# A fused recurrence and token/channel mixer on one core: the same operations in another fixed order per engine

## The chip, the core and the metric

The kernel runs on one core of one Trainium2 chip. The metric is the device time of one execution in microseconds. Besides the times there is one profiled execution, with a trace of every instruction: TensorE (PE; its weight loads are shown as PEld), VectorE (DVE), ScalarE (ACT), GpSimd (POOL), SyncE (SP), and the DMA queues.

## What is computed

Four batches, eight heads, 768 positions, head size 48. A gated linear recurrence gives y, and y, with its heads side by side as 384 columns, goes through a mixer over positions (768 to 256 to 768) and one over channels (384 to 1536 to 384). Cut to what matters:

```python
f = 1.0 / (1.0 + np.exp(-f_logit))
for t in range(S):
    state = f[:, :, t, :, None] * state + np.einsum('bhd,bhe->bhde', k[:, :, t], v[:, :, t])
    y[:, :, t] = np.einsum('bhd,bhde->bhe', q[:, :, t], state)
...
xt = x.transpose(0, 2, 1)                      # x is y with heads joined
h = np.maximum(xt @ w_tok1, 0.0) @ w_tok2
u = x + h.transpose(0, 2, 1)
return u + np.maximum(u @ w_ch1, 0.0) @ w_ch2
```

Inputs and the output are fp32; the kernel computes with bf16 operands and fp32 sums.

## The kernel before

**Tiling.** Positions are cut into six chunks of 128 per batch. For a chunk, the logarithms of the gates (ScalarE: exp, then ln; lines 366 and 367, in batch 0 lines 387 and 383) are split into a high and a low bf16 part (the low one by a subtraction on GpSimd or VectorE, line 374, batch 0 line 396) and summed over positions by two matmuls with a triangle of ones (lines 456 and 457). ScalarE takes exp of the sums, once with each sign, into `GG` (lines 466 and 468); VectorE multiplies q and k by it (line 485, "product" in the prediction; batch 0 line 629) into `qk`; `qk` is transposed, for batches 0 to 2 by TensorE (line 495, batch 0 line 636) and a copy into `qkT`, for batch 3 by a DMA transpose on SP's queue (line 498). The scores of a chunk (line 408) are masked by VectorE into `AmT` (line 536); the state products k·v are line 424 (batch 0: line 657). The state goes on by `tsum` and `state` on VectorE (lines 547 and 549, 544 for the first chunk), with the chunk's last gate `glast`, which a small DMA on SP's queue lays out (line 476). Two copies "spread" each half of the state into the block-diagonal `state_bd` (ScalarE line 344 or GpSimd line 348). The result y of a chunk is one PSUM bank: state part (line 556) and masked scores times v (line 560). It is copied twice, to bf16 `x_bf` and fp32 `x_nat`. Batch 0 takes its chunks two at a time with masks for pairs (lines 607 to 736).

**Mixer.** Per batch: tok1 (line 750) with relu into `h1T`, tok2 (line 766), u added into `x_nat` (line 782) and cast to `u_bf`, six times three transposes into `uT` (line 798), 24 blocks ch1 of three matmuls (line 814), each relu'd by ScalarE (line 352) or VectorE (line 354) into `zT`, then per 128 positions three blocks ch2 of four matmuls (line 832), the sum (line 838) and the store (line 842).

**Order.** Nothing is scheduled when the kernel is built. The code makes a list of 1073 operations with their needs; the string `ORDER` says in which order they are recorded, and each engine takes its own in that order. In `ORDER` a token is an operation's number; a letter behind it chooses the engine where there is a choice (A ScalarE, D VectorE, G GpSimd); a number behind a colon is the PSUM bank (there are eight) that the operation opens; `z` and a number are that many idle matmuls (line 863), which only keep TensorE going. Engines, DMA queues and banks hence work strictly in the order of the list; an instruction that waits holds up all behind it on its engine. The numbers `kind` of each operation, among them the sizes for loads, are for the program that searches orders; they change no instruction.

**Loads.** GpSimd issues the loads of q, k, v and the weights (line 264, line 270), each with a descriptor run of its own in GpSimd's queue. Batches 1 and 2 have one load of the gate logits f and 18 of a chunk of k, q or v each; batch 3 has four, one each of f, k, q and v in one piece. Three load buffers for q, k, v and two for f turn round over the batches.

## Time and profile before

| | us |
|---|---|
| three runs | 175.95, 176.18, 178.95 |
| median | 176.18 |
| the profiled execution | 175.42 |
| its span, first to last instruction | 173.7 |
| TensorE busy | 165.0 |
| VectorE busy | 128.9 |
| ScalarE busy | 115.0 |
| GpSimd busy | 81.4 |

The profiled execution's own time holds 1.7 us outside the span. Times in the views are microseconds from the span's start. A row of a timeline has start, length, engine, line, operation, output and inputs, and how many equal instructions are merged; in brackets stands the engine's idle time just before it and what ended it. A row of a group has the line, form and count, then the busy time, the mean length of one in ns, and the idle time before the group with what ended it. Matmul records overlap, since the next one starts while the last still runs through the array.

### The profile page before, as it was taken

What the parts mean: (1) busy time and instruction counts of PE and PEld (TensorE: products, weight loads), DVE (VectorE), ACT (ScalarE), POOL (GpSimd) and SP (SyncE); (2) the same over time, 40 slices, a digit from 0 to 9 for tenths busy, and PEclk for the clock granted to TensorE, in tenths of its full rate; (3) what the DMA queues carried; (4) which work ended last, traced back from release to release, by engine and by line L of the source; (5) the groups of instructions that cost most, each with busy time, mean ns of one, the idle gap of its engine ahead of it and who ended that gap; (6) DMA issues with size and microseconds to landing.
All of it is one profiled execution on the core that took longest, in us unless ns stands there. A gap on an engine that the chain in (4) does not pass through costs nothing.

```text
span 173.7 us, 4503 instructions
## 1 busy us (share of the span) xinstructions
PE 165.0 (95%) x1795; PEld 104.5 (60%) x1795; DVE 128.9 (74%) x285; ACT 115.0 (66%) x258; POOL 81.4 (47%) x104
## 2 busy tenths in 40 slices
PE   6989988999999999999799999999999999999991
PEld 2466654656666766766567655666666657556660
DVE  7979985896798979799997967887938284555142
ACT  3999958999983598998958766797853234233000
POOL 2997814999772998999938401400000021000000
PEclk9999999999999999999999999999999999999999
DMA  5999999999999998999999968643270001210154
GB/s 142 228 170 177 250 209 199 142 99 189 162 137 236 95 107 186 165 158 125 79 143 133 107 33 101 207 84 86 41 131 0 0 0 49 109 72 0 38 193 183
DMA packets 84837, 21.56 MB, mean 124 GB/s; under 512 B 77552, under 2 KB 84000, under 8 KB 84816
## 3 DMA queue, kind: packets, MB, share of 16 engines
q0 software_dynamic: 69600, 13.77, 92.3%
q1 hardware_dynamic: 15216, 7.51, 17.2%
q8 instruction: 14, 0.23, 0.6%
q14 instruction: 7, 0.06, 0.1%
HBM read 25.17 MB, written 4.72 MB: 172 GB/s over the span
## 4 chain that ended last, share of the span: by engine, by line
PE 79%; ACT 10%; DVE 5%; DMA 2%; issue 1%; DVEq 0%; ACTq 0%
PE ps L832 26%; PE ps L814 24%; PE ps L750 5%; PE ps L766 4%; PE ps L408 3%; PE ps L798 2%; PE ps L495 2%; DMA f_sb<-in_f_logit_dram 2%; PE ps L863 2%; PE ps L560 2%; PE ps L456 2%; DVE zT L354 2%; PE ps L424 1%; PE ps L556 1%; ACT L L383 1%; ACT f_sb L387 1%
## 5 line engine op out<-in xcount | busy, mean ns | idle before, releaser
L832 PE MATMUL ps<-w_ch,zT 128*128 128x384 bf16 (+2 forms) x300 | 54.3, 319 | 0.0
L814 PE MATMUL ps<-uT,w_ch 128*128 128x384 bf16 x288 | 51.6, 326 | 1.0 <-DVE x_bf L346 1.0
L814 PEld LDWEIGHTS <-w_ch 128*128 128x128 bf16 x288 | 27.3, 98 | 18.3 <-issue 1.5
L832 PEld LDWEIGHTS <-zT 128*128 128x128 bf16 x300 | 27.7, 98 | 16.3 <-issue 0.4
L352 ACT ACTIVATE zT<-ps 128x384 bf16<-128x384 f32 x56 | 26.0, 498 | 13.7 <-PE ps L814 13.0
L354 DVE TENSOR_SCALAR zT<-ps 128x384 bf16<-128x384 f32 x40 | 21.1, 552 | 8.1 <-PE ps L814 7.4
L536 DVE TENSOR_TENSOR AmT<-ps,tri_bf 128x512 bf16<-128x512 f32 x36 | 23.5, 684 | 2.2 <-PE ps L408 2.2
L348 POOL CAST state_bd<-state 48x192 bf16<-48x192 f32 x18 | 6.5, 360 | 35.0 <-DVE state L549 16.5
L838 DVE TENSOR_TENSOR x_nat<-x_nat,ps 128x384 f32<-128x384 f32 (+2 forms) x25 | 13.1, 534 | 10.3 <-PE ps L832 9.9
L264 POOL DMA_DIRECT2D v_sb<-in_v_dram x16 | 15.9, 1000 | 1.3 <-DMA w_ch<-in_moe_w_ch_dram 1.0
L264 POOL DMA_DIRECT2D qk_sb<-in_q_dram x16 | 16.0, 999 | 0.1
L264 POOL DMA_DIRECT2D qk_sb<-in_k_dram x16 | 15.8, 996 | 0.2
L348 POOL CAST u_bf<-x_nat 128x384 bf16<-128x384 f32 x10 | 5.3, 532 | 19.9 <-DVE x_nat L782 19.9
L782 DVE TENSOR_TENSOR x_nat<-x_nat,ps 128x384 f32<-128x384 f32 x21 | 11.1, 549 | 3.5 <-PE ps L766 3.4
L750 PE MATMUL ps<-x_bf,w_tok 128*128 128x384 bf16 x48 | 13.5, 326 | 0.2 <-ACT x_bf L344 0.2
L374 POOL TENSOR_TENSOR Llo<-L 128x384 bf16<-128x384 f32 x13 | 11.0, 848 | 3.0 <-ACT L L367 2.8
L485 DVE TENSOR_TENSOR qk<-qk_sb,GG 128x768 bf16<-128x768 bf16 x18 | 11.5, 644 | 0.9 <-ACT GG L468 0.9
L344 ACT ACTIVATE state_bd<-state 48x192 bf16<-48x192 f32 x22 | 7.9, 360 | 6.2 <-DVE state L549 5.8
L863 PE MATMUL ps<-steady 128*128 128x512 bf16 x27 | 9.8, 476 | 1.5 <-DVE steady L279 1.5
L344 ACT ACTIVATE x_bf<-ps 128x384 bf16<-128x384 f32 x15 | 7.3, 487 | 5.5 <-DVE zT L698 2.0
L766 PE MATMUL ps<-h1T,w_tok 128*128 128x384 bf16 x48 | 10.2, 325 | 0.6 <-ACT h1T L352 0.6
L468 ACT ACTIVATE GG<-ps 128x384 bf16<-128x384 f32 x18 | 8.9, 496 | 0.5 <-PE ps L457 0.5
(99 smaller groups left out, 275.0 us busy)
## 6 DMA issues: line engine op xcount, KB each, us to landing
out_dram<-x_nat SPq DMA_DIRECT2D x23, 192.0 KB, 2.0
f_sb<-in_f_logit_dram POOLq DMA_DIRECT2D x3, 1152.0 KB, 11.3
f_sb<-in_f_logit_dram SPq DMA_DIRECT2D x3, 384.0 KB, 4.1
w_ch<-in_moe_w_ch_dram POOLq DMA_DIRECT2D x2, 576.0 KB, 11.5
qk_sb<-in_k_dram POOLq DMA_DIRECT2D x12, 96.0 KB, 4.5
qk_sb<-in_q_dram POOLq DMA_DIRECT2D x12, 96.0 KB, 5.0
v_sb<-in_v_dram POOLq DMA_DIRECT2D x12, 96.0 KB, 4.6
w_ch<-in_moe_w_ch_dram POOLq DMA_DIRECT2D x1, 1152.0 KB, 10.1
```

Source lines behind the costliest of these rows:

```text
L264: lambda eng=eng, into=into, of=of: eng.dma_start(out=into, in_=of),
L344: nc.scalar.activation(out_, in_, AF.Copy, bias=0.0, scale=1.0)
L348: nc.gpsimd.tensor_copy(out_, in_)
L352: nc.scalar.activation(out_, in_, AF.Relu, bias=0.0, scale=1.0)
L354: nc.vector.tensor_scalar(out_, in_, 0.0, None, ALU.max)
L536: add(("masked", b, c, p), DVE, lambda half=half, made=made: nc.vector.tensor_tensor(half, made(), tb4, ALU.mult), need=["tri_bf"], make=[ ...
L750: add(("tok1", b, rt, kt), PE, lambda rt=rt, kt=kt, pm=pm: nc.tensor.matmul(banks[pm.at][:, 0:DM], lhsT=w_tok1[:, kt, rt * 128:(rt + 1) * ...
L766: nc.tensor.matmul(banks[pm.at][:, 0:DM], lhsT=w_tok2[:, kt, tt * 128:(tt + 1) * 128], rhs=h1T[:, kt, :], start=(kt == 0 and not held), st ...
L814: nc.tensor.matmul(banks[pm.at][:, 0:384], lhsT=w[:, kt, c0:c0 + 128], rhs=uT[:, kt, cols], start=(kt == 0), stop=(kt == 2))
L832: nc.tensor.matmul(banks[pm.at][:, 0:n1 - n0], lhsT=zT[:, kt, tt * 128:(tt + 1) * 128], rhs=w_ch2[:, kt, n0:n1], start=(kt == 0), stop=(kt ...
L838: add(("sum", b, tt, n0), DVE, lambda un=un, pm=pm, n=n1 - n0: nc.vector.tensor_tensor(un, un, banks[pm.at][:, 0:n], ALU.add), make=[("x_n ...
L863: nc.tensor.matmul(banks[NBANK - 1], lhsT=steady[:, 0:128], rhs=steady, start=True, stop=True)
```

## The change

`ORDER` is replaced as a whole. It holds the same operations; one idle matmul more (28 for 27). Engines differ where there is a choice: of the two-way operations, six spreads of the state go from ScalarE to GpSimd; two copies of `qkT` and three of `uT` go from ScalarE to VectorE; two `x_bf` and two `x_nat` copies go from VectorE to ScalarE; one `u_bf` from ScalarE to GpSimd, one low part from GpSimd to VectorE, one relu of `h1T` and one of `zT` from ScalarE to VectorE, one u copy from VectorE to ScalarE. Banks are dealt anew. The order of the loads in GpSimd's queue changes (batch 3's k in one piece moves ahead of the last two q chunks of batch 2, for instance), and the stores of batches 0 and 1 stand later in SP's queue, all of them behind batch 3's first two transposes.

Some constants (`steady`, `inc2`, `exc2`, `half2`, `pmask`) lie in the buffer `x_nat[2]`, which is written as such only from batch 2 on, and no longer in tiles of their own. The rest are names and settings that choose what was chosen before (`NQ = 2`, `TURNED` with all six chunks of batch 3, `UTURN` empty) and the search's own numbers for a load in one piece (5900 for f, 5100 for the others).

```diff
+UTURN = ()
+NQ = 2
...
-TURNED = (3,)
+TURNED = {(3, 4), (3, 1), (3, 0), (3, 3), (3, 2), (3, 5)}
...
 ORDER = """
-32 33 13 17 34 20 5 10 18 21 6 14 22 0 7 1 9 36 12 15 49 23 35 26 2 3 28 51 24 25 37 50 53D 54 52D 39 27 z13 105:0 55
+32 33 21 22 11 34 5 7 17 14 19 0 15 1 35 12 20 24 23 49 6 2 36 3 4 26 28 18 50 25 39 8 51 52D 54 53D 37 27 z13 105:0
...
-1039 1070 1044 1071 1072 1050 804 1045 1051 570 1055 829 1046 1059 1047 1056 1040 1057 1060 1052 1041 1042 1061 1062
+1060 1070 1049 1071 1061 1072 1065 1062 1050 1066 829 1039 1051 1067 1045 1052 1040 824 1046 1047 1041 1042
...
-    def at(b, c):
+    def at(c):
 
-        return c % 2
+        return c % NQ
...
-            size = (1210 if n == "f" else 1150) if paired else (930 if n == "f" else 730) * many
+            size = (1210 if n == "f" else 1150) if paired else (930 if n == "f" else 730) * many if many < NCH else 5900 if n == "f" else 5100
...
-    steady = st([128, 512], BF16, "steady")
+    spare = x_nat[2].rearrange("p c n -> p (c n)").bitcast(BF16)
+    steady = spare[:, 0:512]
...
-        inc2 = st([128, C], BF16, "inc2")
-        exc2 = st([128, C], BF16, "exc2")
-        half2 = st([128, 2], BF16, "half2")
-        pmask = [st([128, C // 2, 2], BF16, f"pmask{j}") for j in range(2)]
+        inc2, exc2, half2 = spare[:, 512:640], spare[:, 640:768], spare[:, 1024:1026]
+        pmask = [spare[:, 768 + j * C:768 + (j + 1) * C].rearrange("p (t j) -> p t j", j=2) for j in range(2)]
...
-        if b in TURNED:
+        if (b, c) in TURNED:
...
+        if b in UTURN:
+            for tt in range(NCH):
+                add(("ut", b, tt), SP, lambda tt=tt: nc.sync.dma_start_transpose(
+                    out=uT[:, :, tt * 128:(tt + 1) * 128], in_=u_bf[:, tt, :]), need=[("u_bf", tt)],
+                    make=[("uT", tt, d) for d in range(3)], kind=("xfer", 700, 2700))
+        for th in range(0 if b in UTURN else 2):
```

## The prediction

> **What bounds the kernel now.** I read the page's shares first, then its slices, then the chain of waits, and then the timeline of each engine round the places where TensorE stops. The page gives the shape:

> ```profile
> span 173.7 us, 4503 instructions
> PE 165.0 (95%) x1795; PEld 104.5 (60%) x1795; DVE 128.9 (74%) x285; ACT 115.0 (66%) x258; POOL 81.4 (47%) x104
> PEclk9999999999999999999999999999999999999999
> ...
> L814 PE MATMUL ps<-uT,w_ch 128*128 128x384 bf16 x288 | 51.6, 326 | 1.0 <-DVE x_bf L346 1.0
> ...
> L485 DVE TENSOR_TENSOR qk<-qk_sb,GG 128x768 bf16<-128x768 bf16 x18 | 11.5, 644 | 0.9 <-ACT GG L468 0.9
> ```

> TensorE is busy for 95% of the span at a full granted clock, so an order can give back only its idle time: 173.7 - 165.0 = 8.7 us. That understates what its stops cost, since records of matmuls overlap. In the chain of waits (start, length, what):

> ```profile
> 19.47 0.65 PE ps L863 x3
> ...
> 148.81 8.78 PE ps L814 x54
> ...
> 169.84 0.56 DVE x_nat L838
> ```

> 54 matmuls in 8.78 us start every 0.163 us, and the page's row for line 814 gives one as 0.326 us long, so a stop shows 0.16 us less idle time than it costs. Three idle matmuls in 0.65 us are 0.22 us each. Behind the last matmul, from 169.8 on, lie 3.9 of the 8.7 us. The stops that I can name, from TensorE's timeline (start, length, what; in brackets the idle time and what ended it):

> ```profile
> 12.63 0.40 PE L636 MATMUL ps<-ident,qk 128*128 128x128 bf16 x4 [0.53 <-DVE qk L629]
> ...
> 22.96 0.30 PE L668 MATMUL ps<-zT 48*64 48x128 bf16 x6 [0.55 <-issue]
> ...
> 28.51 0.65 PE L766 MATMUL ps<-h1T,w_tok 128*128 128x384 bf16 x3 [0.65 <-ACT h1T L352]
> ...
> 75.19 0.62 PE L408 MATMUL ps<-qkT 48*128 48x128 bf16 x16 [0.17 <-ACT qkT L344]
> ...
> 85.90 0.65 PE L814 MATMUL ps<-uT,w_ch 128*128 128x384 bf16 x3 [1.00 <-DVE x_bf L346]
> ...
> 102.70 0.32 PE L750 MATMUL ps<-x_bf,w_tok 128*128 128x384 bf16 x1 [0.20 <-ACT x_bf L344]
> ```

> With 0.16 us added to each they cost 0.69, 0.71, 0.81, 0.33, 1.16 and 0.36 us, 4.1 us together. Behind 103 us nothing of that size is left. None is ended by a load. Who waited for the loads of line 264 at all:

> ```profile
> who waited for it (us, times):
>   ACT f_sb L387: 2.2, 1
>   DVE qk L629: 0.3, 1
> ```

> Both lines are batch 0's (387 and 629 stand in its code alone). No engine that computes waited for a load of batches 1 to 3. So what the new order was searched for, patience with the loads of batches 2 and 3, removes no stall of this execution; what counts is what else the new order does.

> **The change part by part.** Every operation stays; the new list has 28 idle matmuls for 27: +0.22 us.

> The stop at 12.63. The transposes of the second pair's q waited for a product on VectorE. TensorE's timeline just before it, and ScalarE's copy beside it:

> ```profile
> 10.31 0.32 PE L610 MATMUL ps<-Llo,inc 128*128 128x384 bf16 x1
> 10.67 0.44 PE L657 MATMUL ps<-v_sb,qk 64*64 64x48 bf16 x32
> 11.04 1.07 PE L636 MATMUL ps<-ident,qk 128*128 128x128 bf16 x16
> ```
> ```profile
> 11.92 1.02 ACT L344 ACTIVATE zT<-ps 128x1024 bf16<-128x1024 bf16 x1
> ```

> The new order does the first pair's 16 transposes (0.9 us from the first start to the last end's place in the stream) before the state products of line 657 (11.04 - 10.67 = 0.37), and then chunk 4's sums (4 x 0.163 = 0.65) and two score blocks, all ahead of the transposes that waited. So this wait goes. What is late next is the first score block, which needs the copy at 11.92: TensorE comes there at 10.31 + 0.16 + 0.9 + 0.22 (an idle matmul) + 0.37 + 0.65 = 12.6, and the copy ends at 12.94. I take 0.3 us of the 0.69 as left: -0.4 (bounds -0.69, and +0.3, were the copy to begin 0.6 us later than in the old order).

> The stop at 85.90 is the dearest. Line 814's block for batch 1 needs a PSUM bank that batch 2's first result holds until VectorE has copied it. VectorE then, and GpSimd beside it:

> ```profile
> 79.70 1.06 DVE L485 TENSOR_TENSOR qk<-qk_sb,GG 128x768 bf16<-128x768 bf16 x1
> ...
> 81.62 0.54 DVE L346 COPY x_nat<-ps 128x384 f32<-128x384 f32 x1
> 82.08 1.01 DVE L354 TENSOR_SCALAR zT<-ps 128x384 bf16<-128x384 f32 x2
> 83.01 1.07 DVE L485 TENSOR_TENSOR qk<-qk_sb,GG 128x768 bf16<-128x768 bf16 x1
> ...
> 84.48 0.90 DVE L549 TENSOR_TENSOR state<-tsum,glast 128x192 f32<-128x192 f32 x1
> 85.31 0.55 DVE L346 CAST x_bf<-ps 128x384 bf16<-128x384 f32 x1
> ```
> ```profile
> 79.53 0.82 POOL L374 TENSOR_TENSOR Llo<-L 128x384 bf16<-128x384 f32 x1
> 80.30 0.91 POOL L264 DMA_DIRECT2D v_sb<-in_v_dram  x1
> 81.21 3.09 POOL L264 DMA_DIRECT2D qk_sb<-in_q_dram  x2
> 84.30 0.86 POOL L374 TENSOR_TENSOR Llo<-L 128x384 bf16<-128x384 f32 x1
> ```

> VectorE runs without a gap (an operation starts some 0.08 us before the record of the last one ends), and from the fp32 copy of that bank at 81.62 to the bf16 one at 85.31 it is 3.7 us. A product of line 485 takes 1.06 here; its 18 took 11.5 us together, so the others are about 0.55. In the new order the fp32 copy goes to ScalarE. Behind the mask that the result needs, VectorE has one more mask (0.60, from its row below less the overlap), two state steps and a uT copy (0.27 each by the state's row of 0.35 further down), three zT copies (0.47 each), one product (0.47, or 0.98) and the bank's copy (0.47): 3.8 to 4.3 us. TensorE comes back to the bank after the result's own 12 short matmuls, seven blocks of line 814 (7 x 0.49) and two pairs of sums (0.33 each), over 4.1 us, and it starts that result only when the mask is there. So the copy comes just in time: I take 0.2 us of the 1.16 as left, -0.95; bounds -1.16 and, with two doubled operations more (0.5 each), 0.

> The stop at 102.70 waited for the last chunk's bf16 copy, behind an fp32 copy of the same bank on VectorE. In the new order VectorE makes the bf16 copy first, and TensorE has a block of four, two sums and two more matmuls (8 x 0.163 = 1.3 us, 0.3 more than before) between the result and its reader: -0.36 (bounds -0.36 and 0).

> The stops at 22.96, 28.51 and 75.19 stay: the first is ended by nothing that the profile shows, at the second relu still sits between the same two layers, and at the third both transposed copies of batch 2's first chunks now go to VectorE, 0.69 us (row below) for ScalarE's 1.02 (the like row at 11.92), but one after the other. 0, bounds -0.7 and +0.7.

> Engines. Six spreads of the state go from ScalarE to GpSimd, two copies of qkT and three of uT from ScalarE to VectorE, four copies of results the other way; the rest are single ones. From the groups of instructions kept apart by shape:

> ```profile
> L536 DVE TENSOR_TENSOR AmT<-ps,tri_bf 128x512 bf16<-128x512 f32 x36 | 23.5, 684 | 2.2 <-PE ps L408 2.2
> ...
> L346 DVE COPY qkT<-ps 128x1024 bf16<-128x1024 bf16 x7 | 4.7, 685 | 2.0 <-PE ps L495 2.0
> ...
> L348 POOL CAST state_bd<-state 48x192 bf16<-48x192 f32 x18 | 6.5, 360 | 35.0 <-DVE state L549 16.5 <-DVE state L544 8.5 <-PE ps L814 4.0
> ```

> A spread is 0.36 us, so GpSimd gets 2.2 us more in its queue and VectorE about 1 us more. None of it is on TensorE's path while each is ready in time; the price where it isn't is in the rivals.

> Loads. Batch 3's k in one piece now goes ahead of two q chunks of batch 2:

> ```profile
> qk_sb<-in_k_dram POOLq DMA_DIRECT2D x12, 96.0 KB, 4.5
> ...
> qk_sb<-in_k_dram POOLq DMA_DIRECT2D x1, 576.0 KB, 9.0
> ```

> Chunks behind a piece come some 4.5 us later (9.0 - 4.5). Nobody waited for them before, and by how much they were early no row here says. Batch 3's gate logits stay where they were among the loads round them. I take 0, bounds 0 and +1.0.

> Stores of batches 0 and 1 are pushed behind batch 3's transposes on SP's queue; nobody waits for them but batch 3's rewriting of x_nat: 0, bounds 0 and +0.5. The end stays: last block of line 832, one sum (0.56 us, the row at 169.84), one store. 0.

> New waits. An order has places that I can't see from the old trace, the transposes of batch 3 above all, whose first use had next to no room. I put +0.4 for them, between 0 and +1.5 (a stop like the dearest here and a small one).

> Sum: 0.22 - 0.4 - 0.95 - 0.36 + 0.4 = -1.1 us, a span of 172.6. The profiled execution took 175.42 us with its 173.7 of span, so 174.3; it lies 0.76 below the median of 176.18, so on that scale 175.1.

> **The rivals.** (1) Contention eats the gain. The product of line 485 takes 1.06 at 79.70, beside GpSimd's subtraction, for 0.55 elsewhere; the state step at 84.48 takes 0.90 beside another, for 0.35 at 95.88 (row below). The new order gives GpSimd seven more operations that read SBUF and takes one away, and VectorE has no slack just where the 1.16 us are to be won. If three of VectorE's operations double there again, on top of its 1 us more work, the -0.95 becomes nothing, and a small stop comes back: about 0 in all, 176.2. For it: the doubled rows. Against it: most spreads follow a state step, when VectorE has gone on to masks from PSUM. [...]

> (2) Slower: spreads stuck behind loads. GpSimd takes its queue in order. Batch 2's fourth state is now spread by GpSimd alone, behind the one-piece load of batch 3's v, and with a subtraction between the two halves:

> ```profile
> 93.42 2.26 POOL L264 DMA_DIRECT2D v_sb<-in_v_dram  x1
> 96.39 0.34 POOL L348 CAST state_bd<-state 48x192 bf16<-48x192 f32 x1 [0.71 <-PE ps L408]
> ```
> ```profile
> 95.88 0.35 DVE L549 TENSOR_TENSOR state<-tsum,glast 128x192 f32<-128x192 f32 x1
> ```
> ```profile
> 98.34 0.33 PE L556 MATMUL ps<-state_bd,qkT 128*128 128x96 bf16 x4
> ```

> The reader starts 2.1 us behind the state's end. If that load starts as the state ends, the second half is there after 2.26 + 0.34 + 0.82 (a subtraction, as at 79.53) + 0.34 = 3.8 us: 1.7 us late. Batch 1's fourth state stands behind four chunk loads in the same way, 4 x 0.91 + 2 x 0.34 = 4.3 us, with the same room 2.2 us late. It decides where the loads are issued so late that less than 1.7 and 2.2 us of them lie ahead of the state. Both together, with my other terms: -1.1 + 3.9 = +2.8, 179.0. Against it: the old order had the row at 93.42 run 2.5 us ahead of the state.

> (3) All six stops go and none comes: 0.22 - 4.1 = -3.9, 172.3.

> **How the numbers follow.** The forecast has a chance of 0.5 (its own bounds 173.6 to 175.9), contention 0.22, stuck spreads 0.18, all stops gone 0.1. The range of 172.8 to 178.6 leaves out most of (3) and the upper half of (2). About 2% (172.7 and 179.7) is what a measurement here tells from no change. Faster by more takes nearly every stop: 0.12. Slower by more takes rival (2) with 0.7 us of unseen waits on top: 0.10. Within: 0.78.

> **What would show it.** The stop of line 814 near 84 to 86 us under 0.4 us, none near 12.6, and ch2's last block ending near 168.7 show the steps right. A line 556 matmul waiting for GpSimd's state_bd shows (2); products of line 485 near 1.06 us and a line 814 matmul waiting for VectorE show (1). Any wait for a load of batch 2 or 3 makes my zero for the loads wrong.

## The result, and the profile after

The new order is slower by half a per cent: 176.38 us in the median of 17 runs (175.87 to 178.35), beside 175.90 for 17 runs of the kernel before (175.15 to 178.95). The ratio of the two is 1.0052, with a 95% interval from 1.0027 to 1.0076. That ratio leaves out six slow executions of before, at 178.46 to 178.95 us, and none of after's; over all 17 of each the means are 176.75 and 176.68 us. The forecast was 1.1 us faster; by the ratio it came out some 0.9 us slower, by the medians and the two profiled executions 0.5. So the loss is small and shows in the usual execution, not in the mean; that the gain of 1.1 us did not come is clear. The profiled execution took 175.93 us (before: 175.42), 174.2 of them in its span.

The page after, its span, TensorE's row, the granted clock and the queue q8, which the experiments take for the one that brings TensorE's own instructions:

```profile
span 174.2 us, 4492 instructions
...
PE 163.8 (94%) x1791; PEld 105.0 (60%) x1796; DVE 129.1 (74%) x288; ACT 110.6 (63%) x249; POOL 82.8 (48%) x110
...
PEclk9999999999999999999999999999999999999999
...
q8 instruction: 14, 0.23, 0.6%
```

TensorE's timeline, the rows with a stop ahead of them in the first 31 us (in brackets the idle time and what ended it):

```profile
17.71 0.50 PE L712 MATMUL ps<-v_sb,zT 64*128 64x48 bf16 x25 [0.50 <-issue]
...
22.19 0.32 PE L712 MATMUL ps<-v_sb,zT 64*128 64x48 bf16 x12 [0.25 <-DVE zT L699]
...
23.96 0.43 PE L712 MATMUL ps<-v_sb,zT 64*128 64x48 bf16 x20 [1.45 <-issue]
...
30.25 0.97 PE L767 MATMUL ps<-h1T,w_tok 128*128 128x384 bf16 x5 [0.65 <-DVE h1T L355]
```

Two groups that answer to those shown of before, from the groups of instructions kept apart by shape (busy time, mean ns of one, idle time before them):

```profile
L820 PE MATMUL ps<-uT,w_ch 128*128 128x384 bf16 x288 | 52.2, 326 | 0.0
...
L486 DVE TENSOR_TENSOR qk<-qk_sb,GG 128x768 bf16<-128x768 bf16 x18 | 10.9, 608 | 0.0
```

Three things are to be seen. Line 820, 814 before, no longer waits for VectorE's `x_bf`. The stop of 0.76 us at 22.96, which "issue" ended before, is now one of 1.63 us from start to start at 23.96, and a second of 0.68 us stands at 17.71. Both cut one operation in two: the 32 small matmuls of line 712, which wait for nothing in the middle. And between 73 and 104 us, where before had the stops at 75.19, 85.90 and 102.70, TensorE's timeline shows no stop at all. At the place of the dearest it has now:

```profile
84.70 0.65 PE L820 MATMUL ps<-uT,w_ch 128*128 128x384 bf16 x3
85.19 1.06 PE L496 MATMUL ps<-ident,qk 128*128 128x128 bf16 x16
86.08 1.14 PE L820 MATMUL ps<-uT,w_ch 128*128 128x384 bf16 x6
```

To see where time goes between two orders, I put beside each operation's start on TensorE the issue time of all operations ahead of it. The issue time of each kind is taken from the trace of before, from its first matmul to the next operation's first, at the lower third of equal ones; an idle matmul counts 0.216 us of work. What a stretch takes beyond that is lost there:

| stretch | lost before, us | lost after, us |
|---|---|---|
| to instruction 191 (11.1 and 12.2 us) | 3.79 | 4.05 |
| from there to instruction 703 (22.96 and 23.97 us) | 1.86 | 3.10 |
| to the first transpose for the channel mixer (31.4 and 33.0 us) | 1.45 | 1.31 |
| to the last half of batch 1's token mixer (about 65 us) | 0.80 | 0.56 |
| to the last matmul | 2.75 | 1.51 |
| all, and TensorE's work | 10.65 and 159.15 | 10.53 and 159.37 |
| last matmul to the end of the span | 3.85 | 4.26 |

The two executions differ by 0.22 us of work, -0.12 of losses and 0.41 at the end, 0.5 in all, as their times do. So the rest of the kernel does gain 1.2 us. The start takes 1.2 us more between two places that I name by the number of TensorE's instruction (two for each matmul, its weights and its product), and the end 0.4 us more. The experiments ask whether that holds, and why.

### The profile page after: what moved, and what is told of

Same layout as the page of the kernel before. It is cut to its first block, busy times and chain, and to the rows that moved or that the text cites. A ratio compares the mean times of both kernels' runs of the same rounds, so it can differ in the third digit from the quotient of the medians.

```text
span 174.2 us, 4492 instructions
## 1 busy us (share of the span) xinstructions
PE 163.8 (94%) x1791; PEld 105.0 (60%) x1796; DVE 129.1 (74%) x288; ACT 110.6 (63%) x249; POOL 82.8 (48%) x110
## 4 chain that ended last, share of the span: by engine, by line
PE 84%; ACT 6%; DVE 3%; issue 2%; DMA 2%; ACTq 0%
PE ps L820 27%; PE ps L838 27%; PE ps L751 5%; PE ps L767 5%; PE ps L496 3%; PE ps L409 3%; PE ps L804 2%; PE ps L561 2%; DMA f_sb<-in_f_logit_dram 2%; PE ps L457 2%; PE ps L425 2%; PE ps L458 2%; PE ps L557 2%; DVE zT L699 2%; ACT f_sb L388 1%
## 5 line engine op out<-in xcount | busy, mean ns | idle before, releaser
L838 PE MATMUL ps<-w_ch,zT 128*128 128x384 bf16 (+2 forms) x300 | 54.0, 320 | 0.0
L820 PE MATMUL ps<-uT,w_ch 128*128 128x384 bf16 x288 | 52.2, 326 | 0.0
L838 PEld LDWEIGHTS <-zT 128*128 128x128 bf16 x300 | 28.1, 98 | 16.7
L820 PEld LDWEIGHTS <-w_ch 128*128 128x128 bf16 x288 | 27.2, 97 | 17.1 <-issue 0.4
L353 ACT ACTIVATE zT<-ps 128x384 bf16<-128x384 f32 x55 | 25.1, 491 | 10.8 <-PE ps L820 10.3
L355 DVE TENSOR_SCALAR zT<-ps 128x384 bf16<-128x384 f32 x41 | 21.3, 552 | 11.7 <-PE ps L820 9.8
L349 POOL CAST state_bd<-state 48x192 bf16<-48x192 f32 x24 | 9.1, 379 | 29.9 <-DVE state L550 22.8
L349 POOL CAST u_bf<-x_nat 128x384 bf16<-128x384 f32 x11 | 5.4, 505 | 19.7 <-DVE x_nat L783 19.6
L345 ACT ACTIVATE state_bd<-state 48x192 bf16<-48x192 f32 x16 | 5.7, 358 | 10.0 <-DVE state L550 7.3
L486 DVE TENSOR_TENSOR qk<-qk_sb,GG 128x768 bf16<-128x768 bf16 x18 | 10.9, 608 | 0.0
L367 ACT ACTIVATE f_sb<-f_sb 128x384 f32<-128x384 f32 x18 | 9.3, 524 | 2.3 <-DMA f_sb<-in_f_logit_dram 2.3
L345 ACT ACTIVATE x_bf<-ps 128x384 bf16<-128x384 f32 x17 | 8.2, 491 | 4.1 <-PE ps L561 2.7
L767 PE MATMUL ps<-h1T,w_tok 128*128 128x384 bf16 x48 | 9.4, 326 | 0.6 <-DVE h1T L355 0.6
L345 ACT ACTIVATE x_nat<-ps 128x384 f32<-128x384 f32 x18 | 8.8, 496 | 1.6 <-PE ps L561 1.2
## 6 DMA issues: line engine op xcount, KB each, us to landing
w_ch<-in_moe_w_ch_dram POOLq DMA_DIRECT2D x2, 576.0 KB, 13.5
```

What stands on the lines that cost most here:

```text
L345: nc.scalar.activation(out_, in_, AF.Copy, bias=0.0, scale=1.0)
L349: nc.gpsimd.tensor_copy(out_, in_)
L353: nc.scalar.activation(out_, in_, AF.Relu, bias=0.0, scale=1.0)
L355: nc.vector.tensor_scalar(out_, in_, 0.0, None, ALU.max)
L486: add(("gated", b, c, *names), DVE, lambda n=n: nc.vector.tensor_tensor(qk[it][:, n, :, 0:D], qk_sb[nb][:, n, :, c, :], GG[i][:, n], ALU.m ...
L767: nc.tensor.matmul(banks[pm.at][:, 0:DM], lhsT=w_tok2[:, kt, tt * 128:(tt + 1) * 128], rhs=h1T[:, kt, :], start=(kt == 0 and not held), st ...
```

## The experiments

**Where the time goes.** Two kernels join the lists (e1 and e2). The first takes the first 446 tokens of the old order (about 60 us) and what is left of the new one; the second the reverse, with 452. All joined kernels stand on the text of after; a bank number or two is renamed at the joint.

```diff
 ORDER = """
-32 33 21 22 11 34 5 7 17 14 19 0 15 1 35 12 20 24 23 49 6 2 36 3 4 26 28 18 50 25 39 8 51 52D 54 53D 37 27 z13 105:0
+32 33 13 17 34 20 5 10 18 21 6 14 22 0 7 1 9 36 12 15 49 23 35 26 2 3 28 51 24 25 37 50 53D 54 52D 39 27 z13 105:0 55
...
+458A 448:1 454A 468 87 460 432A 92 333:0 459 325 474
```

> Order of before up to the token mixer of batch 1 (its first 446 tokens, about 60 us), order of after from there on; one bank renamed. Theory: after loses 1.3 us more than before until the first transpose of the token mixer at about 31 us and gains 1.5 us in the rest, and the two are independent; then this kernel is about 1.2 us faster than before (ratio 0.991 to 0.995), the stop of 1.17 us at 85.90 and the one of 0.36 at 102.70 are gone, and the stall at 22.96 is back at 0.7 to 0.8 us. Rival: the gain of the rest comes from loads that the new start issues at other times; then the stops at 86 and 103 stay and the ratio is 0.998 to 1.002.

> The reverse: order of after in its first 452 tokens, order of before from there on; one bank renamed. Theory: about 1.2 us slower than before (ratio 1.005 to 1.009), with the stalls of 0.7 us at about 17.7 and 1.6 us at about 24 of after and the stops of before at 75 to 103. Rival (the two stretches depend on each other): within 0.3 us of after or of before, without the stops at 86 and 103.

Measured: old start, new rest 175.32 us, ratio 0.9981 (0.9951 to 1.0011); new start, old rest 179.18 us, ratio 1.0148 (1.0088 to 1.0208). The first shows the three stops of 75 to 103 us gone, and loses 1.66 us from 65 us on, for 1.51 in after; the second loses 2.74 there, for 2.75 in before. The rest's gain is real and goes with the rest's order alone. But the two don't add up to after by the first theory: with its own gain of 1.1 to 1.2 us the first should have been nearer 0.993, and the second was slower than the theory's 1.009. Something else was in them. In the second it is in part the clock: four of its six executions have a mean granted clock of 0.987 to 0.990 and took 179.08 to 179.36 us; the two at 1.00 took 177.13 and 177.92.

**The end.** In after, in the two joined kernels and in six others of this study 2.14 to 2.17 us lie between the landing of the last store and the end of the span; in before and two others it is 1.73 to 1.74. SyncE closes the program with a row of waits some 0.07 us apart; in after one step of that row takes 0.47 us. The nine kernels have 91 recorded SyncE instructions, the three have 92. So I gave SyncE one more: a store of batch 1 in two halves, once alone (e9) and once with the first kernel's joined order.

```diff
-                add(("store", b, tt, n0), SP, lambda un=un, to=to: nc.sync.dma_start(out=to, in_=un),
+                def store(un=un, to=to, b=b, tt=tt):
+                    for cols in (slice(0, 192), slice(192, 384)) if (b, tt) == (1, 0) else (slice(0, un.shape[1]),):
+                        nc.sync.dma_start(out=to[:, cols], in_=un[:, cols])
+
+                add(("store", b, tt, n0), SP, store,
```

> After, with one store of batch 1 (token tile 0) issued as two halves of 192 columns: one instruction more on SyncE, nothing else. From the landing of the last store to the end of the span it is 1.73 us in before and 2.17 us in after, where SyncE's closing row of waits has a gap of 0.47 us; the two kernels with 92 recorded SyncE instructions and the same end lack the gap, all six with 91 have it. Theory (a page of SyncE's own program ends there, and one instruction more moves that under the wait for the last store): the gap is gone, 1.73 us from landing to end, 0.4 us faster than after (ratio to before 1.000 to 1.004). Rival (something that after stores or waits for last): 2.17 us, ratio as of after.

> The order of before for its first 446 tokens and of after from there on (the first experiment), with one SyncE instruction more by the same split store. If the gap at the end and the start-up are all that separates after from its gain of 1.3 us behind 60 us: 0.5 to 1.1 us faster than before, ratio 0.994 to 0.997. Rival (the gains do not add up): ratio 0.998 to 1.002 as for the first experiment.

Measured: after with 92 instructions has 1.68 us behind the last landing, and 176.17 us, ratio 1.0004 (0.9970 to 1.0039). The joined order with 92 has 1.66 us there, and 174.82 us, ratio 0.9931 (0.9901 to 0.9961): it beats both kernels. Its page and TensorE's rows with a stop near 23 us:

```profile
span 172.9 us, 4500 instructions
...
PE 164.6 (95%) x1795; PEld 104.7 (61%) x1795; DVE 127.6 (74%) x283; ACT 113.1 (65%) x257; POOL 82.5 (48%) x107
```
```profile
22.84 0.30 PE L669 MATMUL ps<-zT 48*64 48x128 bf16 x6 [0.43 <-issue]
```

So the end cost after 0.45 us, and one SyncE instruction mends it. That a page of SyncE's program ends in that row fits what is found below for TensorE. The trace has a second queue of instructions, q14, whose last transfer starts 0.4 to 0.7 us ahead of the end in the nine kernels with 91 and 1.6 to 1.8 us ahead of it in the seven with 92 that end the same way. But it does not say for which engine; the count alone is shown.

**What the stops at 17.71 and 23.96 are.** 128 matmuls lie between the two, 256 instructions, and the 14 transfers of q8 have 16384 bytes each: 14 x 256 = 3584, nearly all of its 2 x 1796 = 3592 instructions. So I took them for places where TensorE had run out of fetched instructions; the 256 instructions of one transfer are called a page of instructions below. If so, they stay at the same instruction when 75 short matmuls are put ahead of everything, and other work meets them.

```diff
-        for _ in range(n):
-            nc.tensor.matmul(banks[NBANK - 1], lhsT=steady[:, 0:128], rhs=steady, start=True, stop=True)
+        for j in range(88 if n == 13 else n):
+            cols = 32 if n == 13 and j else 512
+            nc.tensor.matmul(banks[NBANK - 1][:, 0:cols], lhsT=steady[:, 0:128], rhs=steady[:, 0:cols], start=True, stop=True)
```

> After, with the 13 idle matmuls of 512 columns ahead of the first sums replaced by one of 512 and 87 of 32 columns: 75 matmuls (150 instructions) more in a time when TensorE waits for the first loads anyway. Theory (supply of instructions): the two stalls without a waiting semaphore stay at the same instruction numbers of TensorE (after about 447 and 703 instructions), so 75 matmuls earlier in the work: at the transposes of pair 4 (about 1.5 us) and in the within of pair 4 (about 0.2 us), nothing at the within of chunks 0 and 2; their sum goes from 2.3 to about 1.7 us, the time to 0.3 to 0.6 us below after. Rival (an unseen wait for data, a bank or VectorE): the stalls stay at the within of chunks 0 and 2 with 0.7 and 1.6 us, and the time is that of after.

> Before, with the same 75 matmuls more ahead of the first sums. Theory (supply of instructions): the stall of 0.76 us leaves the scores of chunk 5 and one of about 1.5 us comes 75 matmuls earlier in the work, at the transposes of pair 4; the time is 0.6 to 1.0 us above before. Rival (an unseen wait for data, a bank or VectorE): 0.76 us at the scores of chunk 5 as it was, and the time of before.

Measured: 176.88 us, ratio 1.0051 (1.0019 to 1.0084) for after with them, 176.99 and 1.0071 (1.0031 to 1.0111) for before. In the first, TensorE's timeline has this:

```profile
21.05 0.84 PE L637 MATMUL ps<-ident,qk 128*128 128x128 bf16 x8 [1.18 <-ACT x_bf L345]
```

The stop (1.42 us from start to start) is now ahead of a transpose of line 637, at the same instruction 703, and the next, of 1.05 us, 256 instructions on inside the within of pair 4 (its masked scores times v, line 712). Line 712's matmuls of chunks 0 and 2 run through. The place is settled: it is the instruction's number. The bracket names ScalarE, which is only the last semaphore that came; this is how a stop of this kind hides under another name. What I expected of the times failed. The short matmuls leave the clock low (in the padded before it is full from 10.4 us on, in before from 5.9): in the padded before a sum of 384 columns follows the other every 0.31 us until 10 us, where before has 0.165, so its first state products come 1.4 us late. That is most of its loss, and its own stop shrank to 0.41 us and moved on by a page, against the 1.5 us expected at instruction 703.

What a page costs with nothing else going on was measured behind the last matmul of after:

```diff
-        for _ in range(n):
-            nc.tensor.matmul(banks[NBANK - 1], lhsT=steady[:, 0:128], rhs=steady, start=True, stop=True)
+        cols = 32 if n == 768 else 512
+        for _ in range(n):
+            nc.tensor.matmul(banks[NBANK - 1][:, 0:cols], lhsT=ident if n == 768 else steady[:, 0:128],
+                             rhs=ident[:, 0:cols] if n == 768 else steady, start=True, stop=True)
...
+ z768
```

> After, with 768 matmuls of 32 columns behind its last one; their results are read by nobody. Theory (supply of instructions): the first ones follow each other in 60 ns or less, and after every 128 of them, at instructions 256 apart, TensorE stands until a page of 16384 bytes has landed, about 1.4 us after the end of that transfer; 128 matmuls take 5.5 to 6.5 us in the long run, where they would issue in 1.8 to 4 us. Rival (stalls at 17.7 and 24 us came from what the matmuls of batch 0 read or write): all 768 at one even pace without stalls, and no pause at the landings of pages.

Measured: the 768 start every 0.025 us, 128 of them in 3.2 us; from the fourth page's end on there is a stop of 0.28 us at each, 256 instructions apart (182.05, 185.50 and 188.96 us), so a page takes 3.45 us. So a page has a price of its own, but a smaller one than expected: 3.45 us there, and 5.6 to 6.6 us from 447 to 703 in the kernels of this study that stop there beside a full load queue. The transfers of instructions in the trace, with the passing of the page ends, show the parts:

| kernel | passes 447 | transfer behind it | goes on at 703, stop |
|---|---|---|---|
| before | 17.11 | 20.09 to 21.43 | 22.96, 0.76 |
| after | 17.71 | 21.17 to 22.50 | 23.96, 1.63 |
| after, padded | 15.38 | 18.71 to 19.67 | 21.05, 1.42 |
| pace, a later page | 178.61 | 179.65 to 180.57 | 182.05, 0.28 |

Each time TensorE goes on 1.4 to 1.5 us behind the end of a transfer; what differs is how long the transfer is in coming, 1.0 us in the pace kernel, 3.0 to 3.5 us in the start.

**Why it is in coming so long.** The first guess was the load traffic, above all the two loads of w_ch1, which after issues at 17.4 us and before at 19.35 and 20.99. One kernel issues them later in after; the other gives before a load more.

```diff
-177 147 62 151:5 126A 123
-133A 189:5 46 185 181 155:2:4 163 183 190 128A 184 134 47 160 186:6 191A
-z1 154:2:1 64 157 136A 158
+177 147 62 151:5 126A 123
+133A 189:5 185 181 155:2:4 163 183 190 128A 184 134 160 186:6 191A
+z1 154:2:1 157 136A 158
...
-197 167A z1 194:1 63 209 196
+197 167A z1 194:1 46 47 64 63 209 196
```

> After, with the two loads of w_ch1 (and the one of q behind them on GpSimd) issued at about 25 us, ahead of the load of k, in place of 17.4 us. Theory (the fetch of instructions stands behind the loads' traffic: from passing a page's end to the start of the next transfer 3.2 to 3.6 us in this stretch, 1.0 us in the quiet end of the pace kernel): the fetch behind instruction 447 starts less than 2.5 us after it, the stall at instruction 703 falls from 1.6 to under 0.7 us, and the kernel is 0.5 to 1.2 us faster than after, unless the weights then come late for the first channel block at 34 us. Rival (the fetch is as slow without that traffic): lag 3.3 us or more and a stall of 1.4 to 1.7 us as before.

```diff
-            lambda: nc.gpsimd.dma_start(out=dst, in_=src.rearrange("(kt p) n -> p kt n", p=128)),
+            lambda: (nc.gpsimd.dma_start(out=dst, in_=src.rearrange("(kt p) n -> p kt n", p=128)),
+                     name == "w_tok2" and nc.gpsimd.dma_start(
+                         out=w_ch2[:, 0:6], in_=moe_w_ch2[0:768].rearrange("(kt p) n -> p kt n", p=128))),
```

> Before, with one load more on GpSimd's queue right behind the one of w_tok2 at about 18.5 us: 1.2 MB of w_ch2 that are loaded again later. Theory (load traffic delays the instruction fetch): the lag of the fetch that starts at 20.1 us in before grows from 3.0 to 3.6 us or more, the stall at instruction 700 from 0.76 to 1.3 us or more, and the time by 0.5 to 1.5 us. Rival: lag and stall as in before; only GpSimd's later issues move by 0.8 us, and the time is that of before within 0.3 us.

Measured: later loads in after (e10) 179.35 us, ratio 1.0174 (1.0138 to 1.0211), a lag from passing 447 to the transfer of 3.37 us and a stop of 1.63; one load more in before (e12) 176.33 us, ratio 1.0019 (0.9983 to 1.0056), a lag of 2.89 us and a stop of 0.57. Both went against the theory (the first also loses 1.25 us where a state is spread late, and its clock is at 0.985 to 0.990 in all six executions). But neither had changed what the DMA engines carried at the time: 219 to 263 GB/s between 19 and 23 us in all four kernels, because loads issued long before were still queued. (In after's view of DMA issues from 14 to 24 us, the load of batch 1's logits takes 11.9 us to land.) A third kernel takes the queue itself away: the logits, w_ch1 and the first q go out only at 24.5 us.

```diff
-177 147 62 151:5 126A 123
+177 147 151:5 126A 123
...
-197 167A z1 194:1 63 209 196
+197 167A z1 194:1 62 46 47 64 63 209 196
```

> After, with the loads of batch 1's gate logits (1152 KB), of w_ch1 (two of 576 KB) and of batch 1's first q all issued behind the spreads of batch 0's fourth state, at about 24 us, in place of 13.4 to 19.7 us. The tenth and twelfth kernels did not change what the DMA engines carried at the time (222 to 263 GB/s between 19 and 23 us in all of them, since loads issued before were still queued), so this one takes the queue itself away. Theory (the pages of instructions wait behind queued loads): between 18 and 22 us the engines carry much less, the page behind instruction 447 starts under 2 us after TensorE passes it (3.2 to 3.8 us in after and e9), the stop at instruction 703 is under 0.8 us; the kernel as a whole is several us slower, since batch 1's logits come late. Rival (the fetch is that slow by itself): lag over 3 us and a stop of 1.4 us or more with the engines quiet.

Measured: 181.64 us in one execution, as batch 1's logits come late. Busy time by stretches, after and then this kernel (the last three columns are the granted clock, the share of a DMA engine, and GB/s):

```profile
19.00:21.00 2.00, 1.95 (x36) 1.28 (x34) 1.85 (x5) 1.85 (x3) 1.49 (x3) 1.00 1.12 254
21.00:23.00 2.00, 1.26 (x46) 0.81 (x46) 2.00 (x5) 1.34 (x4) 0.06 (x1) 1.00 1.00 219
23.00:25.00 2.00, 1.04 (x28) 0.80 (x27) 1.60 (x3) 0.14 (x1) 0.05 (x1) 1.00 1.09 208
```
```profile
19.00:21.00 2.00, 2.00 (x37) 1.24 (x34) 1.99 (x5) 1.99 (x3) 0.69 (x2) 1.00 1.03 178
21.00:23.00 2.00, 1.66 (x62) 0.99 (x62) 2.00 (x5) 1.30 (x4) 0.00 (x0) 1.00 0.06 10
23.00:25.00 2.00, 2.00 (x46) 1.25 (x39) 1.92 (x4) 0.74 (x2) 0.83 (x2) 1.00 0.03 8
```
```profile
22.82 0.42 PE L713 MATMUL ps<-v_sb,zT 64*128 64x48 bf16 x20 [0.34 <-issue]
```

The engines fall quiet just before 21 us. The page behind 447 still comes 2.9 us after its end was passed, more than the 2 us expected, but it starts at 20.59 as the queue runs dry, takes 0.94 us for 1.33 in after, and the stop at 703 is 0.53 us for 1.63. The next page, in a quiet queue, starts 1.14 us behind 703 (3.6 us in after). So with the queue gone the page comes early; the moved and added loads couldn't show it, since the queue was full either way (219 to 263 GB/s, for 10 from 21 to 23 us here). That is one execution, and busy engines alone don't make a page late: in the padded before the transfer behind 447 starts 1.47 us after 15.12, with 170 GB/s from 15 to 17 us. There the long load of batch 1's logits had only begun to be issued, at 14.94 us (14.00 in before, where 447 is passed at 17.11). Which of the queued loads a page waits for was not tested.

**Is the stop free for other work, and what does it do to the clock?** If TensorE has nothing to execute there, six idle matmuls ahead of the stop (1.3 us, 12 instructions) cost next to nothing. And they should keep the clock up: in three profiles with the new start (e2, e9, e10) the granted clock falls to one half 0.6 to 1.8 us after the stop at 703 ends. After with one SyncE instruction more (e9), by stretches:

```profile
22.00:24.00 2.00, 0.51 (x13) 0.24 (x13) 2.00 (x5) 0.34 (x1) 0.00 (x0) 1.00 1.01 209
24.00:26.00 2.00, 1.77 (x45) 1.20 (x45) 0.60 (x2) 0.74 (x2) 0.68 (x2) 1.00 1.14 210
26.00:28.00 2.00, 2.00 (x40) 1.36 (x41) 0.71 (x2) 0.66 (x3) 1.93 (x4) 0.51 1.18 216
28.00:30.00 2.00, 2.00 (x18) 1.30 (x15) 1.02 (x2) 0.90 (x4) 2.00 (x3) 0.63 1.14 204
30.00:32.00 2.00, 1.35 (x8) 0.64 (x7) 0.51 (x2) 1.37 (x6) 0.48 (x1) 1.00 1.75 177
```

Its mean clock is 0.99; (0.49 + 0.37) x 2 us lost at half speed make a stretch of 3.4 us. The same stretches of after's profile have 1.00 throughout, so the page's row of nines was one case of two. Of after's 17 runs three have a mean clock of 0.986 to 0.990, and took 177.69 to 178.35 us. This is no mark of the new order, though: of the 107 executions of before that ran beside the first fourteen experiments eight have 0.987 to 0.990, at 178.33 to 179.00 us. Where the clock falls in those no profile shows.

```diff
-129A z1 161:2:3
+129A z1 z6 161:2:3
```

> After with one SyncE instruction more (the split store of e9), and with six idle matmuls of 512 columns (0.216 us each, 1.3 us in all) ahead of the within of pair 2, where after stands 1.6 to 1.9 us at instruction 703. Theory (at that place TensorE has run out of fetched instructions, and a stop of that length makes its granted clock fall to half for about 3.4 us in some executions: 4 of 10 of e9 show a mean clock of 0.986 to 0.990 and 177.1 to 177.6 us): the six cost under 0.3 us in the executions at full clock, the stop shrinks to under 0.8 us, no execution has a mean clock under 0.992, and the ratio to before falls to 0.996 to 1.000. Rival (the stop is a wait of another kind, or the clock falls for another reason): 1.0 to 1.3 us more, ratio 1.005 to 1.008, or the low clocks stay.

Measured: 175.83 us, and no execution of 12 has a mean clock under 0.996. TensorE's rows:

```profile
22.11 1.46 PE L873 MATMUL ps<-x_nat 128*128 128x512 bf16 x6 [0.16 <-issue]
...
23.98 0.50 PE L712 MATMUL ps<-v_sb,zT 64*128 64x48 bf16 x26 [0.22 <-issue]
```

It goes on at 23.98 us, as after did at 23.96: 1.3 us of idle matmuls cost nothing up to there, and the stop shrank from 1.63 to 0.41. So the first half of the theory holds. The second fits, no more: no low clock in 12 executions, beside four in ten of e9 and three in 17 of after, but on another chip than e9's, where before had two in 23. The ratio, 1.0027 (1.0003 to 1.0051), missed the 0.996 to 1.000 expected, and doesn't differ from e9's by more than the intervals.

What holds the clock in the old start was seen with the old order for all of batch 0's attention and the new one from there (the joint at token 200), with its 13 idle matmuls in that stretch (e5) and without them (e8):

```diff
-213 221 215D 214A 222A 223D
+213 221 215D 214A 222A 223D 64 63 65 342 339 224:4
...
-z1
-z3
```

> Order of before for its first 200 tokens (all of batch 0's attention and the first half of its token mixer, to about 28 us), order of after from there on; two banks renamed. Theory (the cost lies in the start, where TensorE's instructions are fetched in pages of 256 at about 6 us each and after reaches the first page's end 1.2 us later; the gain lies behind 60 us): 0.7 to 1.3 us faster than before, ratio 0.993 to 0.997, one stall of about 0.7 at instruction 700 and none of 1.6. Rival (the orders fit only their own start, as the first exchange hinted with 0.3 us lost at the joint): ratio 0.998 to 1.005.

> The kernel with the order of before up to token 200 and of after from there, without its 13 idle matmuls (26 instructions) between 12.8 and 28 us; what the others compute is as it was. Theory (supply of instructions): the page ends come 4 and 9 matmuls of real work later, which is worth 0.2 to 0.4 us to the same kernel with them, if the granted clock stays at 1.00. Rival: they lie in waits and cost nothing, ratio to that kernel 0.999 to 1.001; or the clock falls without them, and it is 0.5 us or more slower.

Measured: 176.42 us with them, ratio 1.0012 (0.9974 to 1.0050), and 177.91 without, ratio 1.0034 (0.9987 to 1.0081). With them nine of the ten executions compared have a mean clock of 0.995 to 1.000 (two more took 194.33 and 336.01 us); without them none has more than 0.989 (one, the profiled one, took 476.30 us at 0.35). So the second rival of e8 had the clock right: the idle matmuls hold it. The time is less sure, since the two intervals overlap. e5 missed its 0.993 to 0.997. Its profile stops for 1.18 us at instruction 700, and its first page ends at 11.98 us for 11.05 in before, though the two have the same order there. Batch 0's first k is what comes late, as the two rows of VectorE show, of before and of e5:

```profile
9.42 0.63 DVE L629 TENSOR_TENSOR qk<-qk_sb,GG 128x384 bf16<-128x384 bf16 x2 [0.26 <-DMA qk_sb<-in_k_dram]
```
```profile
10.26 0.63 DVE L630 TENSOR_TENSOR qk<-qk_sb,GG 128x384 bf16<-128x384 bf16 x2 [0.76 <-DMA qk_sb<-in_k_dram]
```

Of the eight unpadded profiles with the old order there, five have this load landed at 9.24 to 9.51 us and pass instruction 191 at 11.03 to 11.18; three (e1, e5 and e14 below) have it landed at 10.17 to 10.42 and pass at 11.98 to 12.86. So executions of one start differ by 1 us or more; why the load lands in two ways stays open.

**What the new order packs into the pages.** From instruction 191 to 703 TensorE takes 11.85 us in before and 11.73 in after. The work in it (issue times as above) is 9.99 us in before, 8.63 in after and 9.83 in after with six idle matmuls. The pages come at much the same pace, and the new order has them hold more of batch 0's shortest matmuls: 189 of them and 32 transposes, where before has 171 and 47. But 0.65 us of the 1.36 between 9.99 and 8.63 are idle matmuls, ten in before and seven in after. Two joined orders asked whether the first 17 or 20 us make the difference:

```diff
-132G 162 183 133A 45 185
+132G 162 183 133A 45 185 189:7 46 155:4:0 163 190 128A
...
-191A 169 158 z3 155:6:2 66
+191A 169 158 z3 155:6:2 66 47 160 159 188A 64 z3
```

> Order of before for its first 126 tokens only (to the first within, about 17 us), order of after from there on; three banks renamed. Theory, if what costs is the late end of the first page of instructions (12.2 us in after, 11.05 in before): 0.7 to 1.2 us faster than after, so ratio 0.996 to 1.000 to before, with instruction 703 at about 23.0 us. Rival, if what costs is the order between 17 and 31 us: the time of after, ratio 1.003 to 1.007, and a stall of about 1.6 at instruction 703 near 24 us.

> The order of before for its first 145 tokens (about 20 us), that of after from there on, one bank renamed, with the split store: what e6 was to show, without its waits on the bank of the idle matmuls. Between instructions 191 and 703 TensorE takes 11.9 us in before and 11.7 us in after, but the work in them is 10.0 us in before and 8.6 us in after. Theory (pages of instructions arrive at that pace whatever stands in them, so the order that packs more work into a page wins): instruction 703 is reached at about 23.0 us with about 17.1 us of work done, where after has 24.0 and 16.8; the kernel is 0.7 to 1.2 us faster than e9, ratio to before 0.993 to 0.998, with full clocks. Rival (what costs lies behind 24 us, in the order of the token mixer): within 0.3 us of e9, ratio 0.999 to 1.003.

Measured: the joint at 17 us 176.73 us, ratio 1.0043 (1.0006 to 1.0080). In that kernel idle matmuls write over a bank in use, so the scores and the attention result of batch 0's chunk 5 are not the reference's; they also wait for that bank's readers, which spoils what it was for (its profile, of 175.25 us, does pass 703 at 22.97, without a stop). The joint at 20 us is free of that: 174.77 us, ratio 0.9951 (0.9920 to 0.9981), faster than e9 by 0.5% as each compares with before. Its profiled execution took 176.07 us, the upper end of a wide set (173.84 to 176.07 but for one), and reached 703 at 24.8 us with 17.2 us of work, not at the 23.0 expected, since its first k came late:

```profile
10.35 0.63 DVE L630 TENSOR_TENSOR qk<-qk_sb,GG 128x384 bf16<-128x384 bf16 x2 [0.77 <-DMA qk_sb<-in_k_dram]
```

From 191 to 703 its work is 9.9 us, as in before, but the stretch takes it 12.8 us, so 2.9 are lost there, nearly as much as in after (some 0.5 of them waiting for a copy on ScalarE, 1.2 at 703). So the times say that the order up to 20 us decides; that it does so by what stands in the pages fits the sums but is not shown by this profile. How often the first k lands late with a given start was not settled, and places in one profile's first 12 us are good to 1 us or so.

## Why the prediction was wrong

It went wrong in two terms that it set to zero, and right in the one that it thought most about. That the time lies inside its range is owed to the range's width, not to its mechanism.

- **The stop at 22.96, "ended by nothing that the profile shows", kept at 0 with bounds of 0.7 either way.** This is the step that failed. The row was taken for a fixed feature of the place. The stop goes with the instruction's number (703 in after, padded or not) and ends 1.3 to 1.5 us behind a transfer of q8 (the table's rows and the kernel with the emptied queue), so I read it as TensorE out of fetched instructions. The new order, which spends the pages between 191 and 703 on cheaper matmuls, loses 1.24 us more in that stretch (3.10 for 1.86), 0.87 of them in this stop (1.63 for 0.76); a second of the same kind, 0.68 us at 17.71, is new. The bound was 0.7 for three stops together. That the transfer of instructions stands behind queued loads rests on one execution (the next page starts 1.14 us behind 703 in the quiet queue, 3.6 in after); that the new order suffers more because of what it packs into the pages is worked out, not shown. A fall of the clock behind the stop, some 1.7 us each time, can't be charged to the new order, since before has such executions too.
- **"The end stays."** It took 0.41 us more, by one SyncE instruction fewer. The last block, sum and store were as predicted: 1.53 us from the last sum's end to the landing in both. The cost lay behind the landing, where no term of mine looked.
- **The stops at 85.90 and 102.70, -0.95 and -0.36.** Right that both go, and the size nearly: with 75.19 (0.33, held at 0) the three stops were worth 1.85 us, and the kernel from 65 us on loses 1.24 us less, so 0.6 came back in pieces. The kernels with that rest lose 1.2 to 1.9 us there; before and the new start with the old rest lose 2.75. The single moves that the prediction took for the cause were not tested one by one. The engine changes that stand ahead of it are net numbers: by the letters in the two lists 114 operations change the engine, 42 from ScalarE to VectorE and 40 back among them.
- **The stop at 12.63, -0.4.** It went, and as foreseen the first scores stop instead (at 13.61, 0.46 us where 0.3 was taken; the bracket names VectorE's state, not the copy). What was not seen is that the first sums lose 0.4 us at 7 to 8 us. To instruction 191 the new order is 0.26 worse.
- **The 0.4 for unseen waits** stood for waits of data. From 31 us on there was no single one of that size; the new start's losses were, by that reading, waits for instructions, which no row of before had by name.
- **The rivals.** Contention did not take the gain: the products of line 485, now 486, take 608 ns for 644, and two of the 18 are doubled (1.18 at 41.08, 0.92 at 80.38) where three were. That GpSimd's subtraction is what doubles them is not shown: those at 79.70 in before and 80.38 in after ran beside one, but those at 39.12 and 83.01 in before (1.14 and 1.07 us) and at 41.08 in after only beside the issue of loads. The masks from PSUM took 0.68 to 0.69 us in both, also beside spreads and subtractions. Stuck spreads cost TensorE less than 0.2 us at any place. None of the three had the mechanism that decided, though the range held the time.
- **The numbers.** The forecast's own bounds, 173.6 to 175.9, do not come out of its terms, whose bounds add up to 173.5 and 180.4. And rival (2) at 179.0 lies above the range's 178.6 as it stands, without 0.7 us of waits on top.

The signs that the prediction gave would have told: no stop near 84 to 86 or 12.6, but the last block ending at 169.89 for the 168.7 forecast, so the gain was made and lost elsewhere.

## What to carry to other kernels

A stop in the middle of one operation, ended by "issue", is worth a look at where it falls in the instruction count. Here, among short matmuls, the stop at 703 was 0.41 us for 1.63 with six idle matmuls of 0.216 us ahead of it, and 0.53 us with loads held back; no kernel here got faster than before by that alone, and the one with the emptied queue lost 6 us to late loads. An order that only moves work changes what stands at the page ends, and one SyncE instruction more or fewer moved the end by 0.45 us; a gain in one stretch is worth proving by joining two orders. One profile shows one execution: look at the mean clock of all runs before calling a row of nines the clock.
